# Linear attention, then RWKV channel mix: the weights of the gate load in two halves and those of the output product in five pieces, one group is mixed in halves, and the orders of all engines are new

## The chip, the cores and the metric

The kernel runs on one core of one Trainium2 chip. Every time is device time of one execution, in microseconds (us); smaller is better. The core has five engines that run beside each other, each working through its own list of instructions in order: TensorE (PE in the profile: matrix products and transposes, with weight loads, PEld, beside them), VectorE (DVE), ScalarE (ACT), GpSimd (POOL, which here mainly issues loads) and SyncE (SP, which here issues stores). Sixteen DMA engines move data between memory and the core. Products are gathered in PSUM, whose banks hold 512 float32 for each of 128 partitions.

## The reference

Two layers follow each other. The first is an attention without a square matrix. Its inputs q, k and v have 8 batches, 8 heads, 576 positions and 64 channels each:

```python
q_s = exp(q - max(q, axis=-1));  q_s = q_s / (sum(q_s, axis=-1) + 1e-09)   # over the channels
k_s = exp(k - max(k, axis=2));   k_s = k_s / (sum(k_s, axis=2) + 1e-09)    # over the positions
kv  = einsum('bhsd,bhse->bhde', k_s, v)
x   = einsum('bhsd,bhde->bhse', q_s, kv)     # then heads and channels side by side: (8, 576, 512)
```

The second is a channel mix. `x_prev` is x moved by one position, zero at the start of a batch:

```python
xk = mu_k * x + (1 - mu_k) * x_prev
xr = mu_r * x + (1 - mu_r) * x_prev
k  = relu(xk @ w_k)                 # 512 -> 1024
v  = (k * k) @ w_v                  # 1024 -> 512
out = v / (1 + exp(-(xr @ w_r)))    # 512 -> 512, the gate
```

## The kernel before

**Attention.** The work on q, k and v goes by batch b (0 to 7) and group g (0 or 1) of four heads, so there are sixteen such groups, written 00 to 71. For a group three loads of float32 go into one of eleven `raw` buffers each (`load30v0` is v of group 30). Batches 0 and 1 are loaded in halves of 288 KB (`load11k0`, `load11k1`; batch 0's v straight to bfloat16), the others whole, 576 KB. ScalarE takes the exponentials of q and k (`expq`, `expk`, L330) and casts v to bfloat16 (`cast`, L336); these are the last users of a raw buffer. VectorE sums the exponentials over the channels (`rsum`), takes reciprocals and scales q (`scale`). TensorE then runs a block: it transposes the scaled q in PSUM and forms kv (L399) with one column more for the sum over positions. The block is named `TKV20` where it stands alone and `B31` where the product q times kv of the group before it is in it. VectorE takes the reciprocal of the sum (`rz`, L406) and weighs kv (`w`); ScalarE copies the transposed q out (`qt`, L377). Where a group's x is formed alone, the product is named `X11`.

**Mixing.** ScalarE copies x out of PSUM: `xb` takes 512 positions (L545), `xs` the last 64 (L548), which lie in the bank of the neighbouring block. VectorE sets the moved edge (`edge`), takes the difference to the moved x (`diff`), scales it by mu (`sc`, one of each of two halves u of the channels and each of the two mixes) and adds the moved x (`mix310` for xk, `mix311` for xr of group 31). The results lie in two rings for four batches.

**Channel mix.** It goes by units of 512 positions (four and one of 256 to every four batches; 0 to 9), which need not end where a batch ends: unit 1 needs batches 0 and 1, unit 2 batches 1 and 2. A unit has eight tiles of 128 of the 1024 channels, `k00` to `k07` for unit 0 (four products each, L623), each followed by `relu` on ScalarE (L610, 512 columns) and `sq` on VectorE (L614). Then come four tiles of 128 positions: `r02` is the gate's product for tile 2 of unit 0 (four products of 512 columns, L655), `th02` its tanh on ScalarE (L660), `v020` and so on the output product in steps (L675), `o02` the gating on VectorE (L681), and two stores of 128 KB, issued by SyncE (`st`, L691). k, r and v share four banks of PSUM (`mm`). In units 0 and 1 the first four k tiles go in two steps, first the channels of one group (`k12`), then of the other (`k12.2`), so that they can begin before the second group is mixed.

**Weights.** POOL issues the loads of the weights (`weight`, L302), converted to bfloat16: `wk` in four pieces, `wr` whole, `wv` in the four pieces that the constant `WV` cuts (L31).

**The order of the work.** Nothing is scheduled by a program. `ORDER` (L44) lists every step once, and each engine issues its own steps in the order of that list; a step waits on its engine until what it needs is done, and everything behind it on that engine waits with it. The number behind a colon is the buffer that the step takes (`load30v0:0` takes raw buffer 0; `r22:1` takes bank 1 of `mm`); a step that takes a buffer waits until its last users are done. POOL issues loads in the order of the list too, and what is issued lands in that order. Where a bank holds two results that different engines read (`rz31` on VectorE and `xs30` on ScalarE read the same bank), the later one of the list waits for the earlier one:

```python
qt30 B31:1.0 relu20:2 ... k26:0 mix211 xs30:1 rz31:1 mix201 rrec400 ... r22:1 th22:1
```

The change touches `graph` with its inner functions `attention` and `unit`, the function that makes the weights' tiles, and `ORDER`.

Of the kernel before, what the change touches and what calls it, by code (L numbers as in the profile page):

```python
# [30 lines left out]
WV = (0, 2, 4, 6, 8)  # L31
# [49 lines left out]
load61v0:1 rsum500:1 v221 v201 k30:0 th23:3 k33:2 expq510:1 load60v0:10 expq410:0 relu33:2 o20
load61k0:3 relu30:1 v230:1 o22 w40:0 rsum410:2 sq30:1 rrec410 sc3110:2 cast410:1 sc3111 sc3011:1
k42:3 k43:2 relu43:0 rrec500 v231 sq33 expk410:1 o23 qt40:2 k47:0 v210:2 load51v0:9 v211 sc3010
scale410:0 relu42:1 sq42:0 k37:1 k40:3 load70v0:0 mix301 st20.2 expk500:2 relu40:2 cast500:2
B41:1.0 o21 rz41:0 k41:3 sq43 relu47:1 relu37:0 k31:2 w41:1 k34:0 scale500:1 sq40 xb40:1
load61q0:6 xs40 st23.2 sq47 mix311 relu41:2 relu34:1 qt41:0 k32:1 sq41 sq37 rsum510:3 sq34
relu31:2 r40:3 st22.2 relu32:0 k46:0 relu46:1 sq31 st20 st12 qt50:1 sq32 B50:0.1 sq46 rz50:1
# [765 lines left out]
```

## Time and profile before

Three runs took 195.58, 195.68 and 195.82 us; the median is 195.68.

| What | Value |
| --- | --- |
| Profiled execution, its own time | 195.74 us |
| Its span (first to last recorded work) | 194.0 us |
| Around the span | 1.74 us |
| TensorE busy | 183.8 us, 95%, 1807 instructions |
| Its weight loads | 89.8 us, 46%, beside the products |
| VectorE busy | 152.3 us, 79% |
| ScalarE busy | 139.4 us, 72% |
| POOL busy | 41.3 us, 21% |
| Granted clock of TensorE, mean | 0.996 |
| The chain that ended last | TensorE 67%, ScalarE 14%, VectorE 10%, waits for nothing shown 3%, DMA 3% |
| Read from memory, written | 33.56 MB, 9.44 MB |

The busy times are sums over the whole span and hide that it has two parts. Up to about 70 us all of the inputs of batches 0 to 3 have to come in (the DMA engines move 255 to 410 GB/s from 24 to 73 us) and ScalarE and VectorE are nearly full; later the transfers mostly stay under 230 GB/s and TensorE alone is full. A view of waits lists, for an engine, what ended its idle time: engine, operation, line, then what it waited for, with the sum, the number and the longest in us. In the listings of single instructions a row has the start (us from the start of the span), the duration, the engine, the line, the operation with its buffers and shape, and in brackets the idle time ahead of it with what ended it. The buffers' letters are those of the program: `raw_b` is the raw buffer 1, `mm_c` bank 2, `vv_c` the third buffer of casts. For a load, a row of the view of transfers gives the size and the time from issue to landing.

### The profile page before, as it was taken

To read this page: it belongs to the slowest core of one execution; us is meant where nothing else is said; L and a number is where in the kernel's file an instruction comes from. 1 tells how busy PE (TensorE), PEld (TensorE's weight loads), DVE (VectorE), ACT (ScalarE), POOL (GpSimd) and SP (SyncE) were. 2 spreads that over 40 slices of the span, in tenths; PEclk is the share of its full clock that TensorE was granted. 3 is DMA by queue.
4 is the path that set the end of the run, shared out by engine and by line. 5 is a ranking of instruction groups with operands and counts; after the bars stand their busy time and mean duration, and the time that the engine had idled before them with its cause. 6 is when DMAs were issued, how large, how long until landed. Compare 5 with 4: busy or idle time off the path is not lost.

```text
span 194.0 us, 4636 instructions
## 1 busy us (share of the span) xinstructions
PE 183.8 (95%) x1807; PEld 89.8 (46%) x1830; DVE 152.3 (79%) x353; ACT 139.4 (72%) x218; POOL 41.3 (21%) x65
## 2 busy tenths in 40 slices
PE   7798979999999989999999999999999999999991
PEld 2264434444544544555444444444444444444751
DVE  1888983999999999999999999999795824342531
ACT  3778999899999999999899969573444525141440
POOL 8345656544325202430020000000000000000000
PEclk9999999999999999999999999999999999999998
DMA  6999999999999999999996603911207003275813
GB/s 200 309 295 274 323 329 255 405 391 406 410 389 400 408 408 307 316 339 409 170 227 184 144 0 30 202 31 37 53 20 174 19 8 81 48 168 132 195 30 108
DMA packets 23614, 41.86 MB, mean 216 GB/s; under 512 B 9372, under 2 KB 12712, under 8 KB 23592
## 3 DMA queue, kind: packets, MB, share of 16 engines
q0 software_dynamic: 9392, 27.99, 43.9%
q1 hardware_dynamic: 13384, 12.14, 26.1%
q10 hardware_dynamic: 816, 1.44, 2.2%
q8 instruction: 14, 0.23, 0.5%
q14 instruction: 8, 0.07, 0.1%
HBM read 33.56 MB, written 9.44 MB: 222 GB/s over the span
## 4 chain that ended last, share of the span: by engine, by line
PE 67%; ACT 14%; DVE 10%; issue 3%; DMA 3%; SPq 1%; ACTq 0%; DVEq 0%
PE mm_b L675 8%; PE mm_c L675 7%; PE mm_d L675 6%; PE mm_c L623 6%; PE mm_d L623 6%; PE mm_a L623 6%; PE mm_b L623 5%; PE mm_a L675 4%; PE mm_a L655 4%; PE mm_d L655 3%; PE mm_c L655 3%; DMA mu_rows<-in_moe_mu_r_dram 3%; PE mm_b L655 2%; ACT rel_a L610 1%; ACT qt_c L377 1%
## 5 line engine op out<-in xcount | busy, mean ns | idle before, releaser
L675 PEld LDWEIGHTS <-k_a 128*128 128x128 bf16 x168 | 16.1, 98 | 17.3 <-issue 0.2
L655 PEld LDWEIGHTS <-xr 128*128 128x128 bf16 x144 | 13.6, 98 | 18.4 <-DMA wr<-in_moe_w_r_dram 1.5
L675 PEld LDWEIGHTS <-k_b 128*128 128x128 bf16 x128 | 12.1, 98 | 14.6 <-DVE k_b L614 0.3
L655 PE MATMUL mm_c<-wr,xr 128*128 128x512 bf16 x39 | 10.2, 380 | 1.4 <-DMA wr<-in_moe_w_r_dram 1.4
L623 PEld LDWEIGHTS <-wk_bb 128*128 128x128 bf16 x80 | 7.8, 98 | 7.8
L623 PEld LDWEIGHTS <-wk_ab 128*128 128x128 bf16 x80 | 7.8, 98 | 7.8
L655 PE MATMUL mm_a<-wr,xr 128*128 128x512 bf16 x44 | 11.3, 379 | 0.0
L623 PEld LDWEIGHTS <-wk_aa 128*128 128x128 bf16 x80 | 7.6, 98 | 7.9 <-issue 0.2
L623 PEld LDWEIGHTS <-wk_ba 128*128 128x128 bf16 x80 | 7.4, 97 | 7.6 <-DMA wk_ba<-in_moe_w_k_dram 0.2
L610 ACT ACTIVATE rel_b<-mm_a 128x512 bf16<-128x512 f32 (+1 forms) x11 | 5.7, 521 | 5.1 <-PE mm_a L623 4.9
L655 PE MATMUL mm_d<-wr,xr 128*128 128x512 bf16 x33 | 9.1, 380 | 0.2
L610 ACT ACTIVATE rel_a<-mm_d 128x512 bf16<-128x512 f32 (+1 forms) x11 | 6.6, 604 | 3.6 <-PE mm_d L623 2.4
L681 DVE SCALAR_TENSOR_TENSOR th_a<-th_a,mm_c 128x512 f32<-128x512 f32 x4 | 2.7, 687 | 8.2 <-PE mm_c L675 5.4
L610 ACT ACTIVATE rel_c<-mm_d 128x512 bf16<-128x512 f32 (+1 forms) x7 | 3.5, 504 | 6.7 <-PE mm_d L623 6.6
L623 PE MATMUL mm_d<-xk,wk_ab 128*128 128x512 bf16 (+1 forms) x30 | 8.1, 351 | 0.1
L614 DVE TENSOR_TENSOR k_a<-rel_a 128x512 bf16<-128x512 bf16 (+1 forms) x15 | 5.9, 392 | 2.8 <-ACT rel_a L610 2.6
L614 DVE TENSOR_TENSOR k_b<-rel_a 128x512 bf16<-128x512 bf16 x14 | 5.9, 421 | 2.7 <-ACT rel_a L610 2.7
L623 PE MATMUL mm_d<-xk,wk_aa 128*128 128x512 bf16 (+1 forms) x29 | 7.9, 350 | 0.0
L623 PE MATMUL mm_b<-xk,wk_bb 128*128 128x512 bf16 (+1 forms) x26 | 7.5, 371 | 0.1
L623 PE MATMUL mm_b<-xk,wk_ba 128*128 128x512 bf16 (+1 forms) x24 | 7.1, 371 | 0.1
L614 DVE TENSOR_TENSOR k_a<-rel_b 128x512 bf16<-128x512 bf16 (+1 forms) x17 | 6.2, 366 | 0.9 <-ACT rel_b L610 0.5
L345 DVE TENSOR_REDUCE rsum_a<-eq_a 128x9 f32<-128x576 bf16 (+1 forms) x4 | 4.1, 1050 | 3.5 <-ACT eq_a L330 3.5
(350 smaller groups left out, 539.4 us busy)
## 6 DMA issues: line engine op xcount, KB each, us to landing
raw_a<-in_v_dram POOLq DMA_DIRECT2D x3, 576.0 KB, 11.4
out_dram<-th_d SPq DMA_DIRECT2D x12, 128.0 KB, 2.4
out_dram<-th_a SPq DMA_DIRECT2D x12, 128.0 KB, 2.4
out_dram<-th_c SPq DMA_DIRECT2D x10, 128.0 KB, 2.5
out_dram<-th_f SPq DMA_DIRECT2D x10, 128.0 KB, 5.6
raw_k<-in_q_dram POOLq DMA_DIRECT2D x2, 576.0 KB, 9.9
raw_g<-in_k_dram POOLq DMA_DIRECT2D x2, 576.0 KB, 10.6
raw_f<-in_k_dram POOLq DMA_DIRECT2D x2, 576.0 KB, 12.3
```

What stands on the lines that cost most here:

```text
L345: return kn.nc.vector.reduce_sum(out=sums(kn.rsums, u), in_=kn.eqs[eq.index][:, :, u, :], axis=AX.X)
L377: kn.nc.scalar.copy(out=to[:, :, 64:64 + S], in_=kn.whole(slot).bitcast(BF16)[:, :, 0:S])
L610: kn.nc.scalar.activation(out=kn.rels[rel.index][:, 0:n], in_=kn.bank(kf)[:, 0:n], func=ACT.Relu, scale=HALF_ROOT)
L614: kn.nc.vector.tensor_tensor(out=kn.k2s[k2.index][:, fc, 0:n], in0=kn.rels[rel.index][:, 0:n], in1=kn.rels[rel.index][:, 0:n], op=ALU.mult)
L623: kn.nc.tensor.matmul(kn.bank(kf)[:, 0:n], lhsT=kn.wk[fc // 4][ct % 2][:, ct // 2, (fc % 4) * 128: (fc % 4) * 128 + 128], rhs=kn.xs[0][:, ...
L655: kn.nc.tensor.matmul(kn.bank(rps), lhsT=kn.xs[1][:, ct, c:c + 128], rhs=kn.wr[:, ct, :], start=(ct == 0), stop=(ct == CT - 1))
L675: kn.nc.tensor.matmul(kn.bank(vps)[:, 0:width], lhsT=kn.k2s[k2.index][:, ft, 128 * m:128 * m + 128], rhs=wv_of(ft)[:, part], start=(ft == ...
L681: kn.nc.vector.scalar_tensor_tensor(out=kn.ths[th.index][:, part], in0=kn.ths[th.index][:, part], scalar=1.0, in1=kn.bank(vps)[:, 0:width] ...
```

## The change

The load of w_r is two loads of two of its four pieces of 128 channels each, `wr0` and `wr1`, into two tiles, and the r products of unit 0 are two steps: `r02` with the first half for channels 0 to 255, `r02.2` with the second. The later units' r products keep one step and need both halves. The load of w_v has five pieces in place of four (the first two are one piece of 128 channels each, 128 KB as bfloat16), and unit 0's v products follow these cuts, five steps to a tile instead of four.

Group 11 is mixed in halves: `xb11` is two copies (`xb110`, `xb111`) of 512 columns, one for each half of the channels, `diff11` is two, and `mix110` is two (`mix1100`, `mix1101`); `mix111` stays one step. The second step of the first k tiles of unit 1 is cut in two likewise (`k12.2`, `k12.3`), each needing the half of the mix that it reads.

All of `ORDER` is written anew. Batch 1 is loaded q first (`load10q0` before `load10k1`); the order of the eight k tiles, four r tiles and of their relus in unit 0 differs; the whole loads of batches 2 and 3 come in another order, with `load30v0` behind `load50q0`, `load40q0`, `load50v0`, `load40v0` and `load31v0`; `load41v0` stands later, behind `expk510`, into raw buffer 5; ScalarE takes `cast310` before `cast300`; `mix201` stands before `rz31` and `rz31` before `xs30`. The buffers and banks of the steps differ with it. The number of raw buffers and all others stays. In the part of `ORDER` shown here the lines of before stand first, then those of after; the rest of it, for units 3 to 9, differs throughout as well.

```diff
-WV = (0, 2, 4, 6, 8)
+WV = (0, 1, 2, 4, 6, 8)
...
+SPLIT = ((1, 1),)
...
-warm load00k1 load01v late load01k0:3 load10k1:4 wk00 load10v1:5 expq001:0 expq000 wk01
-rsum001:0 ACT!load01k1 rsum000 load10q1:6 expq011:1 rrec001 load10q0 rrec000 rsum011:1 fill:1
...
-wp010:1 cast101:0 load10k0 k02:1 edge01 load10v0 X010:1.0 mucopy x0011 x0100 load11q1 wr k03:0
-expq101:2 expq100 k01:2 expk101:2 x0101 k00:3 k01.2 k02.2 load11v1:8 load11k1:9 k00.2 relu00:0
-k03.2 rsum101:2 wp011 X011:0.1 rsum100 load11k0 sq00:0 load11v0 relu01:1 rrec100 sq01 wv0
-relu02:2 k04:3 wv1 x0110 wv2 k06:2 rrec101 expq110:0 wv3 scale100:2 relu04:0 load20q0:10 expk100
-load30q0:0 load20v0:2 cast100 k07:1 k05:3 scale101 rsum110:3 sq04 rrec110 sq02 relu06:1 relu03:0
-load21q0:1 sq06 x0111 TKV10:0 load21v0:3 relu07:2 r02:2 r03:0 r00:1 rz10:2 load20k0:6 scale110:0
-expq111 relu05:1 w10:0 qt10:2 r01:3 cast111:1 rsum111 expk111:0 expk110 rrec111 scale111 cast110
-B11:1.0 sq03 th03:0 v030:0 th01:1 th00:2 xs10:0 v010:3 sq07 load31q0:4 xb10 rz11:0 w11:1 sq05
-edge10 diff10:0 qt11:0 v000:1 th02:3 v011 v001 sc1000:0 sc1001 v031 X11:0.1 sc1010:1 sc1011 v012
-load21k0:5 v032 v013 xs11:1 v002 mix100 xb11 v033 v003 edge11 expq200:1 diff11:1 expq300:2 o01
-load31k0:7 sc1101:2 v020:2 v021 v022 sc1100 o00 v023 mix110 load41q0:9 o02 rsum200:0 k11:3
-sc1111:0 k12:1 load31v0:8 k12.2 cast200:2 o03 mix101 k10:2 k11.2 k10.2 relu12:0 k16:1 expq210:0
-relu11:2 k17:0 relu16:1 sq12:1 sq11 relu10:0 sc1110 relu17:2 cast210:0 k13:3 rrec200 mix111 st02
-expk200:1 k15:1 k13.2 scale200:1 sq16 r11:2 load30k0:10 k14:0 rsum210:1 sq10 rrec210 TKV20:1
-rz20:1 sq17 relu13:1 load30v0:0 r12:3 th11:4 r10:2 w20:2 sq13 expk210:2 relu14:0 r13:0 qt20:1
-scale210:2 sq14 rsum300:2 load40k0:2 relu15:2 th12:5 sq15 B21:0.1 expq310:1 rz21:2 load51k0:1
-rrec300 v120:1 v110:3 w21:0 st01.2 st00 st02.2 xb20:0 scale300:0 st00.2 xs20 th13:6 load40q0:3
-edge20 qt21:2 rsum310:3 diff20:0 th10:3 v121 load40v0:6 sc2001:2 sc2000 v111 expk300:0 X21:1.0
-r20:0 v130:2 xs21:1 v131 rrec310 xb21 o11 v100:3 edge21 v101 mix200 diff21:1 load60k0:5 o12
-sc2101:1 sc2100 mix210 o10 st01 cast300:1 st03 TKV30:0 cast310:2 th20:2 expk310:1 load50v0:4
-expk400:2 load50q0:10 rz30:0 k27:1 sc2110:0 st11.2 sc2111 relu27:1 o13 expq400:0 w30:1 k20:0
-scale310:1 load41v0:0 load70q0:8 sq27:0 k21:3 relu21:0 k24:1 rsum400:0 k23:2 k22:3 qt30:0
-B31:1.0 relu20:2 sq20 sc2010:2 st11 st12.2 relu23:1 cast400:0 relu24:2 sc2011 sq21 relu22:0
-k26:0 mix211 xs30:1 rz31:1 mix201 rrec400 w31:2 k25:2 scale400:2 sq22 xb30 edge30 qt31:1 sq23
-load50k0:7 load60q0:2 load51q0:3 r22:1 th22:1 st10.2 relu25:0 sq24 diff30:1 r30:3 relu26:1
...
+warm load00k1 load01v late load01k0:3 load10q0:4 wk00 load10q1 expq001:0 expq000 load10k0:5
+rsum001:0 ACT!load01k1 rsum000 wk01 expq011:1 rrec001 wk11 rrec000 rsum011:1 fill:1 fill.2:2
...
+expk010:1 fill.19:3 fill.20:1 fill.21:1 T01:3 kvn00:0 load10v1:6 mu:0 load11q0:7 fill.22:1
+expk011 load10v0 edge00 load10k1 wp000:0 load11q1 wr0 X000:1.0 load11k1:8 wp001 mucopy qt01:1
+expq100:2 KV010:2 x0001 KV011 Z01 rz01:1 kvn01:1 wp010:1 edge01 wr1 load11k0 X001:0.3 x0000
+k01:0 k03:1 x0010 x0011 X010:1.0 x0100 k02:2 wp011 k00:3 x0101 rsum100:2 rrec100 X011:0.1 x0111
+scale100:2 expq101 expk100:2 k01.2 load11v0:9 k00.2 k03.2 rsum101 x0110 relu01:0 k02.2 load11v1
+relu00:1 wv0 wv1 relu03:2 cast101:0 k04:0 k07:3 sq01:0 k05:1 relu04:0 expq110:0 k06:0 rrec101
+cast100 expk101 expq111 scale101 sq00 rsum110:3 sq03 relu02:1 TKV10:0 r02:2 relu06:2 rrec110
+sq02 r01:0 relu05:1 r00:1 rsum111 sq04 expk111:0 rz10:2 wv2 w10:0 rrec111 relu07:0 scale111:0
+wv3 scale110 wv4 load30q0:10 r03:3 load20q0:0 load20v0:2 r01.2 qt10:2 r02.2 sq06 expk110
+load21q0:1 cast110:1 r03.2 r00.2 cast111 load21v0:3 th00:0 sq05 B11:1.0 th03:1 th02:2 xs10:0
+v030:1 v031 rz11:0 v000:3 v010:2 v011 v001 w11:1 sq07 xb10 edge10 qt11:0 v012 diff10:0 sc1000:0
+v032 v002 X11:0.1 xs11:1 th01:3 sc1001 v013 v003 v004 xb110 load20k0:4 v014 sc1011:1 v033 xb111
+load21k0:6 edge11 v020:0 v021 mix100 v034 sc1010 load30k0:5 v022 load50q0:7 v023 v024 diff110:1
+o00 k11:3 diff111 sc1110:2 o01 sc1100:0 expq300:1 sc1101 mix1100 k12:2 load31q0:8 expq200:2
+k12.2 mix1101 k12.3 o02 k11.2 rsum200:0 sc1111 o03 cast200:2 k11.3 k10:0 mix111 st00 relu12:2
+load40q0:9 sq12:1 k10.2 k10.3 relu11:1 sq11 rrec200 mix101 expq210:0 k17:2 k13:3 k13.2 k16:1
+load50v0:10 k13.3 relu10:0 scale200:1 sq10 cast210:0 k15:0 relu17:2 relu13:1 sq13 load40v0:0
+load31v0:2 r11:2 expk200:1 relu16:0 th11:4 r10:3 TKV20:1 rsum210:1 sq17 st03 st03.2 r13:1 k14:2
+load30v0:1 expk210:2 relu15:1 rrec210 rz20:1 w20:2 qt20:1 relu14:2 th13:5 load31k0:3 scale210:2
+r12:0 B21:0.1 v120:2 expq310:2 sq16 sq15 sq14 rsum300:2 rz21:2 st01 load40k0:4 xb20:1 v110:1
+w21:0 th10:6 rrec300 rsum310:3 xs20 qt21:2 v121 edge20 scale300:0 v130:3 load51q0:6 th12:1
+expk300:0 st02.2 load41k0:8 load51k0:5 st00.2 st02 diff20:0 X21:1.0 v111 o12 o11 sc2000:0 xb21:0
+v100:0 xs21 edge21 sc2001 r20:2 v131 cast310:1 cast300:2 diff21:1 v101 mix200 sc2100:2 sc2101
+mix210 sc2010:1 rrec310 o10 o13 TKV30:1 rz30:0 scale310:1 k27:1 th20:0 st13 w30:1 k24:2 k20:0
+sc2110:0 sc2111 expk310:1 expq400:0 expk400:2 relu27:0 relu20:1 k22:3 relu24:2 sq27:0 mix211
+sq24 k21:1 qt30:0 cast400:0 k23:0 relu22:0 st13.2 sc2011 B31:0.1 sq20 rsum400:0 mix201
+load41q0:2 k25:2 xb30:0 st12 k26:3 rz31:1 rrec400 relu21:2 r21:1 relu23:1 r22:0 w31:2 scale400:2
+xs30 qt31:1 th22:2 B40:1.0 sq22 sq21 sq23 load71q0:1 load61q0:3 relu25:0 edge30 diff30:1 v220:0
+load70v0:9 r23:2 st12.2 sc3000:2 xs31:1 relu26:2 load61v0:4 sq25 sq26 xb31 load51v0:0 th21:5
+rz40:2 expk410:0 r30:3 sc3001 edge31 diff31:0 st10.2 st11 st10 v200:1 v221 th30:1 sc3011:0
+sc3101:1 sc3100 expk510:1 mix300 th23:6 expq410:1 mix310 v201 load50k0:8 sc3110:2 o22 o20 k37:3
+k42:2 k30:0 rsum410:1 sc3111 relu37:1 expq500:2 rsum500:2 k33:1 sq37:1 rrec410 relu30:0
+load41v0:5 w40:0 st20.2 scale410:0 k43:3 k40:0 st22 st11.2 mix311 relu33:2 v230:1 expq510:0 v231
...
     wk_done = [[add("POOL", lambda h=h, g=g: weight(kn.wk[h][g], kn.w_k, F, g, 2, 2, 512 * h),
                     name=f"wk{h}{g}") for g in range(2)] for h in range(2)]
-    wr_done = add("POOL", lambda: weight(kn.wr, kn.w_r, C, 0, 1, CT, 0), name="wr")
+    wr_done = [add("POOL", lambda h=h: weight(kn.wr[h], kn.w_r, C, 2 * h, 1, 2, 0), name=f"wr{h}")
+               for h in range(2)]
     wv_done = [add("POOL", lambda i=i, a=a, e=e: weight(kn.wv[i], kn.w_v, C, a, 1, e - a, 0),
                    name=f"wv{i}") for i, (a, e) in enumerate(zip(WV, WV[1:]))]
...
-        def copy_first():
-            kn.nc.scalar.copy(out=kn.xbs[xb.index][:, :, 64:576], in_=kn.whole(pair))
+        halves = (slice(0, 1), slice(1, 2)) if (b, g) in SPLIT else (slice(0, 2),)
+
+        def copy_first(h):
+            kn.nc.scalar.copy(out=kn.xbs[xb.index][:, h, 64:576], in_=kn.whole(pair)[:, h, :])
...
         def then(made, other):
-            evs = [add("ACT", lambda: copy_second(other), [made], [xb], [other], name=f"xs{tag}"),
-                   add("ACT", copy_first, [made], [xb], [pair], name=f"xb{tag}")]
-            o = add("DVE", edge, evs + [late_consts], name=f"edge{tag}")
-            xdiff = add("DVE", diff, [o], [xd], name=f"diff{tag}")
+            last = add("ACT", lambda: copy_second(other), [made], [xb], [other], name=f"xs{tag}")
+            many = len(halves) > 1
+            firsts = [add("ACT", lambda h=h: copy_first(h), [made], [xb], [pair],
+                          name=f"xb{tag}{h.start if many else ''}") for h in halves]
+            o = add("DVE", edge, [last, late_consts] + ([] if many else firsts), name=f"edge{tag}")
+            diffs = [add("DVE", lambda h=h: diff(h), [o, f], [xd],
+                         name=f"diff{tag}{h.start if many else ''}")
+                     for h, f in zip(halves, firsts)]
             for m in range(2):
-                s = [add("DVE", lambda m=m, u=u: scale_x(m, u), [xdiff, mu_done],
+                s = [add("DVE", lambda m=m, u=u: scale_x(m, u), [diffs[u if many else 0], mu_done],
                          [xms[m]], [xd], name=f"sc{tag}{m}{u}") for u in range(2)]
-                mixed[b, g, m] = [add("DVE", lambda m=m: mix(m), s, [], [xms[m], xb], name=f"mix{tag}{m}")]
+                if many and m == 0:
+                    mixed[b, g, m] = [add("DVE", lambda m=m, h=h: mix(m, h), [s[h.start]], [],
+                                          [xms[m], xb], name=f"mix{tag}{m}{h.start}")
+                                      for h in halves]
+                else:
+                    mixed[b, g, m] = [add("DVE", lambda m=m: mix(m, slice(0, 2)), s, [],
+                                          [xms[m], xb], name=f"mix{tag}{m}")]
 
...
+                fine = any((b, 1) in SPLIT for b in bs)
+                for cts in (((0, 2), (1,), (3,)) if fine else ((0, 2), (1, 3))) if step == 4 else ((0, 2, 1, 3),):
                     gs = sorted({ct % 2 for ct in cts})
+                    ready = [o for b in bs for ct in cts
+                             for o in (mixed[b, ct % 2, 0][ct // 2:][:1] if (b, ct % 2) in SPLIT
+                                       else mixed[b, ct % 2, 0])]
                     for i in range(step):
                         fc = f1 + i
                         mms[i] = add("PE", lambda kf=kfs[i], fc=fc, cts=cts: k_part(kf, fc, cts),
-                                      [o for b in bs for g in gs for o in mixed[b, g, 0]]
+                                      list(dict.fromkeys(ready))
                                       + [wk_done[fc // 4][g] for g in gs] + [mms[i]],
                                       [kfs[i]] if cts[0] == 0 else [], [],
                                      name=f"k{index}{fc}")
...
-            def r_part(rps=rps, c=c):
-                for ct in range(CT):
+            def r_part(cts, rps=rps, c=c):
+                for ct in cts:
                     kn.nc.tensor.matmul(kn.bank(rps), lhsT=kn.xs[1][:, ct, c:c + 128],
-                                        rhs=kn.wr[:, ct, :], start=(ct == 0),
+                                        rhs=kn.wr[ct // 2][:, ct % 2, :], start=(ct == 0),
                                         stop=(ct == CT - 1))
...
             own = sorted({4 * half + c // S, 4 * half + (c + 127) // S})
-            r = add("PE", r_part,
-                     [o for b in own for g in range(2) for o in mixed[b, g, 1]] + [wr_done],
-                     [rps], [], name=f"r{index}{m}")
+            ready = [o for b in own for g in range(2) for o in mixed[b, g, 1]]
+            if index == 0:
+                r = add("PE", lambda f=r_part: f((0, 1)), ready + wr_done[:1], [rps], [],
+                        name=f"r{index}{m}")
+                r = add("PE", lambda f=r_part: f((2, 3)), wr_done[1:] + [r], [], [],
+                        name=f"r{index}{m}")
+            else:
+                r = add("PE", lambda f=r_part: f(range(CT)), ready + wr_done, [rps], [],
+                        name=f"r{index}{m}")
...
     kn.wv = [const.tile([128, e - a, C], BF16, name=f"wv_{x}")
-             for x, a, e in zip("abcd", WV, WV[1:])]
-    kn.wr = const.tile([128, CT, C], BF16, name="wr")
+             for x, a, e in zip("abcdefgh", WV, WV[1:])]
+    kn.wr = [const.tile([128, 2, C], BF16, name=f"wr_{x}") for x in "ab"]
```

More of the change, by code (lines that the diff above doesn't have):

```diff
@@ L81 @@
[L81 to L86, printed above, removed]
@@ new lines @@
+fill.13:1 fill.14:2 fill.15:3 fill.16:0 muload wide:0 scale000:0 expq010 expk000:0 rsum010
+expk001 scale001 widecopy wk10 rrec010 fill.17:1 fill.18:2 fill.23:3 fill.24:1 fill.25:2
+fill.26:3 fill.27:1 KV001:0 rrec011 scale010:1 KV000 T00:1 rest Z00 qt00:0 scale011 rz00:0
+expk010:1 fill.19:3 fill.20:1 fill.21:1 T01:3 kvn00:0 load10v1:6 mu:0 load11q0:7 fill.22:1
+expk011 load10v0 edge00 load10k1 wp000:0 load11q1 wr0 X000:1.0 load11k1:8 wp001 mucopy qt01:1
+expq100:2 KV010:2 x0001 KV011 Z01 rz01:1 kvn01:1 wp010:1 edge01 wr1 load11k0 X001:0.3 x0000
@@ new lines @@
+o23 sc3010 st01.2 relu42:1 sq30 v210:2 v211 o21 cast410:2 qt40:2 expk500:2 relu43:0 sq33 B41:0.1
+st21.2 st22.2 sq42:0 sq43 mix301 k41:1 k34:3 load60v0:2 k47:2 xs40:1 xb40 rrec500 relu41:2 sq41
+load60q0:7 relu34:1 relu40:0 k32:1 relu47:2 rz41:0 cast500:1 k46:3 w41:1 sq40 edge40 k36:0 st20
+k31:2 relu32:0 load70q0:6 load61k0:5 k44:1 sq34 relu46:1 scale500:1 sq32 qt41:0 relu36:0 sq46
+sq47 k35:3 rsum510:3 diff40:0 relu35:1 sq35 sc4001:1 r40:0 relu31:2 B50:1.0 st21 k45:3 th40:4
+relu44:1 xb41:0 sq31 sc4011:2 sc4000 r31:2 mix400 sq36 r33:0 v300:1 expq610:1 load71k0:8 th31:3
@@ L553, in edge, with diff @@
             kn.nc.vector.tensor_copy(out=t[:, :, 1:64], in_=t[:, :, 576:639])
-        def diff():
+        def diff(h):
             t = kn.xbs[xb.index]
-            kn.nc.vector.tensor_tensor(out=kn.xds[xd.index][:], in0=t[:, :, 64:64 + S],
-                                       in1=t[:, :, 0:S], op=ALU.subtract)
+            kn.nc.vector.tensor_tensor(out=kn.xds[xd.index][:, h, :], in0=t[:, h, 64:64 + S],
+                                       in1=t[:, h, 0:S], op=ALU.subtract)
         def scale_x(m, u):
@@ L564, in scale_x, with mix @@
                                        scalar1=kn.mu[:, c:c + 1], scalar2=None, op0=ALU.mult)
-        def mix(m):
-            kn.nc.vector.tensor_tensor(out=kn.xs[m][:, g::2, c0:c0 + S],
-                                       in0=kn.xms[xms[m].index][:],
-                                       in1=kn.xbs[xb.index][:, :, 0:S], op=ALU.add)
+        def mix(m, h):
+            kn.nc.vector.tensor_tensor(out=kn.xs[m][:, g::2, c0:c0 + S][:, h, :],
+                                       in0=kn.xms[xms[m].index][:, h, :],
+                                       in1=kn.xbs[xb.index][:, h, 0:S], op=ALU.add)
@@ L633, in unit @@
                 mms = [None] * step
-                for cts in ((0, 2), (1, 3)) if step == 4 else ((0, 2, 1, 3),):
+                fine = any((b, 1) in SPLIT for b in bs)
+                for cts in (((0, 2), (1,), (3,)) if fine else ((0, 2), (1, 3))) if step == 4 else ((0, 2, 1, 3),):
                     gs = sorted({ct % 2 for ct in cts})
+                    ready = [o for b in bs for ct in cts
+                             for o in (mixed[b, ct % 2, 0][ct // 2:][:1] if (b, ct % 2) in SPLIT
+                                       else mixed[b, ct % 2, 0])]
                     for i in range(step):
```

71 lines of the change are left out of this document (31 added, 40 removed).

## The prediction

> **What bounds the kernel now.** I read the waits of TensorE, the chain that ended last from 20 to 72 us, a table of busy time by stretch, then the rows of the places found. First, what TensorE waited for:
>
> ```profile
> PE mm_c L655 <- DMA wr<-in_moe_w_r_dram: 1.4, 1, 1.4
> ...
> PE mm_b L655 <- ACT xb_b L545: 0.7, 1, 0.7
> ...
> PE att_a L489 <- issue: 0.3, 1, 0.3
> ```
>
> After the start that is nearly all. The stretches (PE, PEld, DVE, ACT, POOL busy; clock; DMA share; GB/s):
>
> ```profile
> 24.50:31.00 6.50, 5.07 (x97) 2.60 (x98) 4.33 (x10) 6.38 (x12) 4.32 (x6) 1.00 1.15 299
> ...
> 39.00:56.00 17.00, 16.85 (x208) 8.05 (x210) 16.96 (x33) 16.56 (x23) 6.50 (x9) 1.00 1.04 401
> 56.00:71.00 15.00, 14.23 (x197) 6.67 (x201) 14.15 (x32) 14.70 (x21) 5.06 (x7) 1.00 1.03 403
> 71.00:189.00 118.00, 117.17 (x968) 57.88 (x982) 91.68 (x204) 76.91 (x126) 7.22 (x10) 1.00 0.55 142
> ```
>
> From 71 us TensorE alone is full. Before, ACT has 6.38 of 6.50 us just where TensorE waits for wr; from 39 to 56 DVE and ACT are both full. The chain there has no wait for wr:
>
> ```profile
> 26.92 1.12 ACT qt_c L377
> 28.04 0.58 ACT vv_b L336
> 28.62 1.15 ACT ek_a L330 x2
> 29.77 0.56 ACT vv_b L336
> 30.33 0.50 ACT th_a L660
> ```
>
> ACT then waits for three loads, one landing every 1.5 us, and does not again until 47:
>
> ```profile
> 36.09 1.16 ACT L330 ACTIVATE eq_b<-raw_k 128x1152 bf16<-128x1152 f32 x1 [0.48 <-DMA raw_k<-in_q_dram]
> 37.59 1.16 ACT L330 ACTIVATE eq_c<-raw_a 128x1152 bf16<-128x1152 f32 x1 [0.34 <-DMA raw_a<-in_q_dram]
> 39.10 1.15 ACT L336 CAST vv_c<-raw_c 128x1152 bf16<-128x1152 f32 x1 [0.34 <-DMA raw_c<-in_v_dram]
> ```
>
> So up to 69 us the end is set by ACT and by the line of loads; the wr wait is TensorE idling beside them.
>
> **The change, part by part.**
>
> *wr in halves.* The r products' four tiles take 3.46 us (four of 0.86). The wait of 1.38 goes, but r02, r01, r00, r03 need the banks that relu02, 06, 05, 07 free, and ACT gets there in its own order. From relu01 at about 19.6 (relu00 had 19.98): relus 0.48 a step, half casts and exponentials 0.57; 10v1 has the bytes in front of it that landed by 20.8 before, so nothing waits until expq111 (11q1, 24.2); relu02 ends at 25.4, relu06 25.8, relu05 26.3, then expk111 (landing 26.1), relu07 27.4. TensorE now waits for ACT: r03's first step starts at 27.4, four second steps of 0.43 end near 29.6, B11 starts there, not at 30.26. wr1 lands at about 27.4 (wr: 26.65), in time. KV11 needs cast111, whose load keeps the landing of the last one of batch 1, 29.55, so it starts at 30.3 to 30.6 for 31.00. Lead of TensorE: 0.4 to 0.7. ACT's queue holds the same from relu01 to the third tanh (8 relus, 9 half steps for 8 and one 0.53 copy, 1.05, three tanh: 11.46 us for 11.42), so the lead of ACT is 0.1 to 0.3.
>
> *wv in five pieces.* Same bytes; one more descriptor call on POOL (0.73, row wv_d 0.71), beside a line that lands one transfer per 0.7 to 1.5 us. wv0 to wv4 land at about 30.2, 30.8, 32.0, 33.3 and 34.5; the v steps reach them in that order and just wait for none: 0 to 0.2. I take 0.
>
> *Group 11 mixed in halves.* Two copies of 512 columns (0.48 a step) for one of 1024 (0.90): +0.06 on ACT. Two differences and two sums of 576 for 1152 (0.67): no such row; below by half (0.34), above by the 576-wide cast from PSUM (0.66): 0 to +0.6 for the two pairs; nearest are the 512-wide squares, also bf16, at 0.335, so +0.1. k12's odd steps gain the wait on half the sum only.
>
> All this lies ahead of the loads at 36.06, 37.57 and 39.07. The bytes ahead of them are the same, so ACT starts again at the same three times with the same work, and the lead is given back there. Worth at 39 us: 0 (bounds -0.3, +0.2).
>
> *The order of the loads.* The third batch's load30v0 was the 13th whole load; it is now the 15th, behind 50q0, 40q0, 50v0, 40v0 and 31v0. The 15th of before:
>
> ```profile
> 46.30 0.72 POOL L206 DMA_DIRECT2D raw_b<-in_k_dram  x1 [1.43 <-ACT ek_b L330]
> ...
> raw_b<-in_k_dram POOLq DMA_DIRECT2D x1, 576.0 KB, 12.7
> ```
>
> It landed at 46.30 + 12.7 = 59.0 with all seven stores of the first unit already paid. cast300 therefore starts at 59.0, where these rows show no wait:
>
> ```profile
> 57.08 1.25 ACT L336 CAST vv_b<-raw_a 128x1152 bf16<-128x1152 f32 x1
> 58.14 1.25 ACT L336 CAST vv_c<-raw_i 128x1152 bf16<-128x1152 f32 x1
> ...
> 59.88 0.48 PE L399 MATMUL att_a<-vv_b,ek_a 64*64 64x65 bf16 x36
> ```
>
> Behind cast300 on ACT stand th20, expk310, expq400, expk400, relu27, relu20, relu24, qt30: 59.0 + 1.05 + 0.49 + 3 x 1.05 + 3 x 0.48 + 1.0 = 66.1. KV30 starts at 60.2 for 59.88, and B31, which waits for qt30, at 66.3 for 65.57: +0.7.
>
> *The reciprocal rz31.* Before, rz31 stood behind the copy xs30 of the same bank, and mix201 behind rz31:
>
> ```profile
> 68.22 0.17 DVE L406 RECIPROCAL rz_b<-att_b 128x2 f32<-128x2 f32 x1 [0.68 <-ACT xb_b L548]
> ...
> 69.10 1.04 PE L655 MATMUL mm_b<-wr,xr 128*128 128x512 bf16 x4 [0.67 <-ACT xb_b L545]
> ```
>
> Now mix201 comes before rz31 and rz31 before xs30: -0.67. From B31 to B40 remain 70.93 - 65.57 - 0.67 = 4.69 us and a wait of some 0.1 for a freed bank: B40 at 71.1 for 70.93. Up to here: +0.2.
>
> *After 71 us.* The same products remain. 118.00 - 117.17 is 0.83, mostly records left out; one gap of 0.1 may go. New: load41v0 can be issued only when expk510 frees its buffer, about 76.6 by ACT's steps; the nearest row, issued at 76.67 (raw_k<-in_v), landed 5.5 later, so 82.1, and cast410's turn is at 81.8 to 82.3. 0 to 0.7, of which I take 0.15, as B41 follows with some products between.
>
> Sum: 0 + 0.7 - 0.67 + 0.1 + 0.15 - 0.05 = +0.25 on the profiled execution's 195.74 (span 194.0 and 1.74 around it): 195.99. The median shown is 0.06 lower: **195.95**. The bounds give 195.4 to 196.6.
>
> **A rule weighed.** The last two landings of batch 1's k halves (issued 19.84 and 21.12, 8.3 and 7.7 to landing: 28.1 and 28.8) are 0.7 us apart, so a transfer costs its bytes in this line. Whatever is fixed in a transfer's time in the line is under 0.7. [...]
>
> **Rivals.**
> 1. *The line of loads is not last (faster).* If load30v0 lands 0.5 us or more earlier than its place says, cast300 follows cast310 at 58.5, B31 starts near 65.8, and the 0.67 at r22 is a gain: -0.4, with a lead kept from the r products up to -0.9. For it: the wait on xb_b is plainly gone. Against: 13 landings in a row are 1.5 us apart or more. 195.0 to 195.4, say 195.2. Chance 0.22.
> 2. *load41v0 comes too late (slower).* Its place is the issue at 76 to 77; from a landing past 82.8 cast410 holds qt40 and expk500 up, and TensorE has B41 next: +0.4 to +1.2. For it: 5.5 us for the row issued at 76.67. Against: 4.2 for the one at 75.06. 196.4 to 197.2, say 196.7. Chance 0.24.
> 3. *The transfers have a fixed cost in the line (slower).* Two more of them, at most the 0.7 us of a whole landing each: load30v0 lands at 60.4, everything behind it 1.4 later, 197.3. For it: nothing separates bytes from calls at one size. Against: halves of 288 KB land 0.7 apart and whole loads of 576 KB 1.5, twice the bytes for twice the time. Chance 0.02.
> 4. *It does nothing:* ACT paces everything to 69 us whatever the order, and late loads have slack: 195.7. Chance 0.07.
>
> **How the numbers follow.** My forecast has 0.45; 0.2%, 0.39 us, is about what a measurement can tell from no change. Rival 1 gives 0.19 faster and 0.03 within; the forecast, with bounds from 195.4 to 196.6, 0.27 within and 0.18 slower; rival 4 0.07 within; rivals 2 and 3 slower with 0.26. Faster 0.19, within 0.37, slower 0.44. The range takes in rivals 1 and 2: 195.0 to 196.8.
>
> **What would show it.** No wait for wr; waits of TensorE at L674 (r) on ACT between 25 and 28 us; ACT idle for the loads of raw_c (31v0) and raw_b (30v0) at 57 and 59 us; KV30 at 60.2, B31 at 66.3; no 0.67 before r22; B40 near 71.1. The prediction is wrong if cast300 runs before 58.8, if the three waits at 36 to 39 us have moved, or if TensorE has more than 0.5 us of new gaps after 71 us.

## The result, and the profile after

Eight runs of the changed kernel took 197.37 to 198.12 us, median 197.67; eight of the kernel before have the median 195.69. The ratio is 1.0098, with a 95% interval of 1.0081 to 1.0116: slower by 1.9 us. The forecast was 195.95, with a range of 195.0 to 196.8: the time missed the forecast by 1.7 us and lies outside the range. The profiled execution took 197.56 us, its span is 195.8, 1.82 us over that of before.

Starts of single instructions show where the two traces part (us from the start of the span):

| Start of | Before | After | Difference |
| --- | --- | --- | --- |
| r02, first gate product | 26.70 | 25.50 | -1.20 |
| B11 | 30.26 | 29.90 | -0.36 |
| v030 | 31.41 | 31.05 | -0.36 |
| k11, first product of unit 1 | 38.80 | 38.64 | -0.16 |
| B31 | 65.57 | 66.52 | +0.95 |
| B40 | 70.93 | 71.28 | +0.35 |
| B41 | 84.99 | 85.82 | +0.83 |
| k90, first product of the last unit | 181.17 | 182.34 | +1.17 |
| last gating on VectorE | 190.06 | 191.24 | +1.18 |
| end of the span | 193.96 | 195.78 | +1.82 |

Up to B40 there is little. From B40 to the last gating the changed kernel loses 0.83 us more, and a last 0.64 us goes where no product is left. (That B41 also stands at +0.83 is chance: the new list puts fewer products between B40 and B41 and more behind B41, so the rows in between don't compare the same work.) What TensorE waited for in the changed kernel:

```profile
PE att_a L542 <- ACT qt_c L380: 1.0, 2, 0.8
...
PE mm_c L674 <- ACT rel_b L625: 0.5, 1, 0.5
PE mm_d L674 <- ACT rel_a L625: 0.5, 1, 0.5
PE att_b L402 <- ACT vv_c L339: 0.2, 1, 0.2
```

The waits for wr and for xb_b are gone. Two of 0.5 for banks that relus free (`rel`) stand in place of the first. At r02 the relu ends at 25.45 and wr0 landed at 25.43, so without the relu it would hardly start earlier. New is the wait of 0.8 us for the copy qt_c, which is qt40. The stretches (same columns as in the prediction):

```profile
24.50:31.00 6.50, 5.50 (x120) 2.67 (x114) 4.01 (x10) 6.50 (x12) 5.01 (x8) 1.00 1.17 277
39.00:56.00 17.00, 16.85 (x210) 7.96 (x208) 16.82 (x32) 16.27 (x23) 6.51 (x9) 1.00 1.04 400
56.00:71.00 15.00, 14.47 (x192) 6.97 (x190) 14.87 (x33) 14.46 (x20) 5.06 (x7) 1.00 1.03 397
71.00:189.00 118.00, 117.16 (x973) 57.23 (x972) 90.68 (x202) 76.45 (x127) 7.22 (x10) 1.00 0.53 144
```

In the first stretch TensorE is 0.43 us busier, and ScalarE is now busy for all of it. From 56 to 71 us ScalarE is idle 0.24 us more, where it waits for loads. In the last row TensorE is as busy as before (117.16 for 117.17), but the trace of before had only 1807 records of products, this one 1830. The idle 0.83 of before are many gaps of 0.05 us, as a record left out makes them, and one of 0.16; the 0.84 here are one gap, in front of B41. The chain of waits names it:

```profile
77.46 6.11 DMA raw_f<-in_v_dram
83.57 0.02 issue
83.60 1.15 ACT vv_c L339
84.75 1.03 ACT qt_c L380
85.78 0.04 issue
85.82 0.22 PE att_a L542 x4
```

`raw_f<-in_v` is load41v0: issued at 77.46, landed at 83.57. cast410 waits for it 0.98 us, qt40 stands behind the cast, and B41 behind qt40.

The end of the span is seen in the transfers from 190 to 197 us, by queue (packets, MB, share of 16 engines). Before:

```profile
q1 hardware_dynamic: 240, 0.26, 14.3%
q10 hardware_dynamic: 240, 0.26, 11.2%
```

After:

```profile
q1 hardware_dynamic: 240, 0.26, 14.4%
q10 hardware_dynamic: 240, 0.26, 11.0%
q14 instruction: 1, 0.01, 0.5%
```

The last stores are the same 240 packets on each of two queues. New is one packet of a queue that the profile calls instruction, 8 KB and 0.52 us on one of the DMA engines, at 193.05, while the last stores are on their way; before, that packet came at 185.88. From the start of the last gating to the end of the span it is 4.54 us for 3.90, and to the last landing of a store 3.33 for 2.68. Each store has sixteen landing records, and fifteen of the last store's are where they were, 2.74 us behind the gating for 2.67; one comes 0.58 later.

### The profile page after: what moved, and what is told of

It reads as the page before. It is cut to its first block, busy times and chain, and to the rows that moved or that the text cites. A ratio compares the mean times of both kernels' runs of the same rounds, so it can differ in the third digit from the quotient of the medians.

```text
span 195.8 us, 4659 instructions
## 1 busy us (share of the span) xinstructions
PE 186.1 (95%) x1830; PEld 90.3 (46%) x1830; DVE 152.8 (78%) x355; ACT 138.6 (71%) x219; POOL 42.4 (22%) x67
## 4 chain that ended last, share of the span: by engine, by line
PE 54%; DMA 20%; issue 8%; DVE 7%; ACT 6%; POOL 4%; POOLq 0%; DVEq 0%
PE mm_d L700 7%; DMA raw_b<-in_v_dram 7%; PE mm_a L638 6%; PE mm_c L700 6%; DMA raw_e<-in_q_dram 6%; PE mm_b L638 6%; PE mm_a L700 4%; PE mm_b L700 4%; PE mm_c L638 4%; DMA raw_h<-in_q_dram 4%; PE mm_d L638 4%; PE mm_a L674 4%; PE mm_b L674 3%; DMA raw_f<-in_v_dram 3%; PE mm_c L674 3%
## 5 line engine op out<-in xcount | busy, mean ns | idle before, releaser
L625 ACT ACTIVATE rel_a<-mm_b 128x512 bf16<-128x512 f32 (+1 forms) x8 | 4.6, 574 | 10.6 <-PE mm_b L638 9.9
L638 PE MATMUL mm_a<-xk,wk_aa 128*128 128x512 bf16 (+1 forms) x30 | 8.5, 365 | 0.5 <-ACT xk L502 0.5
L629 DVE TENSOR_TENSOR k_a<-rel_c 128x512 bf16<-128x512 bf16 (+1 forms) x17 | 6.4, 375 | 3.4 <-ACT rel_c L625 3.1
L629 DVE TENSOR_TENSOR k_b<-rel_c 128x512 bf16<-128x512 bf16 x11 | 4.6, 420 | 5.0 <-ACT rel_c L625 5.0
L638 PE MATMUL mm_a<-xk,wk_ab 128*128 128x512 bf16 (+1 forms) x30 | 8.5, 365 | 0.0
L625 ACT ACTIVATE rel_a<-mm_a 128x512 bf16<-128x512 f32 (+1 forms) x10 | 5.9, 592 | 3.0 <-PE mm_a L638 2.7
L674 PE MATMUL mm_c<-wr_a,xr 128*128 128x512 bf16 x22 | 6.5, 379 | 0.5 <-ACT rel_b L625 0.5
L674 PE MATMUL mm_c<-wr_b,xr 128*128 128x512 bf16 x22 | 6.5, 379 | 0.0
L674 PE MATMUL mm_a<-wr_b,xr 128*128 128x512 bf16 x22 | 6.5, 379 | 0.0
L674 PE MATMUL mm_a<-wr_a,xr 128*128 128x512 bf16 x22 | 6.5, 378 | 0.0
```

Of the source, the lines that this page charges most:

```text
L625: kn.nc.scalar.activation(out=kn.rels[rel.index][:, 0:n], in_=kn.bank(kf)[:, 0:n], func=ACT.Relu, scale=HALF_ROOT)
L629: kn.nc.vector.tensor_tensor(out=kn.k2s[k2.index][:, fc, 0:n], in0=kn.rels[rel.index][:, 0:n], in1=kn.rels[rel.index][:, 0:n], op=ALU.mult)
L638: kn.nc.tensor.matmul(kn.bank(kf)[:, 0:n], lhsT=kn.wk[fc // 4][ct % 2][:, ct // 2, (fc % 4) * 128: (fc % 4) * 128 + 128], rhs=kn.xs[0][:, ...
L674: kn.nc.tensor.matmul(kn.bank(rps), lhsT=kn.xs[1][:, ct, c:c + 128], rhs=kn.wr[ct // 2][:, ct % 2, :], start=(ct == 0), stop=(ct == CT - 1))
```

## The experiments

The times below are medians, and each ratio is to the kernel before on the same chip; the changed kernel has 197.67 and 1.0098.

**The late load and the end.** First the two losses that the table shows, singly and together.

```diff
-... v201 load50k0:8 ... relu30:0 load41v0:5 ...
+... v201 load41v0:8 ... relu30:0 load50k0:5 ...
```

> The changed kernel, with load41v0 and load50k0 exchanged in the line of loads (each takes the other's place and buffer); nothing else. Theory (the late load): v of group 41 lands at about 80.2 in place of 83.6, cast410 no longer waits (0.98 us), qt40 and with it B41 come 0.8 us earlier, the gap of 0.84 us of TensorE at 85.8 goes, and the time is 196.7 to 196.9 for 197.6. Load50k0 then lands at 83.6, ahead of expk500's turn at 85. Rival (ScalarE's own order in front of qt40 holds B41): the gap stays and the time is 197.6.

Measured: 196.70 us, ratio 1.0048 (1.0036 to 1.0060). ScalarE with load41v0 landed at 80.08:

```profile
82.24 0.38 ACT L623 ACTIVATE rel_b<-mm_c 128x256 bf16<-128x256 f32 x1
82.50 1.15 ACT L337 CAST vv_c<-raw_i 128x1152 bf16<-128x1152 f32 x1
83.54 1.13 ACT L378 COPY qt_c<-att_b 128x1152 bf16<-128x1152 bf16 x1
84.55 1.19 ACT L331 ACTIVATE ek_c<-raw_f 128x1152 bf16<-128x1152 f32 x1
```

The cast follows at once, B41 starts at 84.91 for 85.82, and the last product 0.98 us earlier. load50k0, which now lands at 83.53, is in time for expk500 (`ek_c`) at 84.55. So of the 1.98 us between the medians, 0.97 are the place of one load.

```diff
     def emit_warm():
+        for _ in range(8):
+            kn.nc.scalar.copy(out=kn.warm[:], in_=kn.warm[:])
         return kn.nc.scalar.activation(out=kn.warm[:], in_=kn.warm[:], func=ACT.Exp)
```

> The changed kernel with eight more copies of one element on ScalarE at its start, where it waits for its first load; nothing else. Theory (the end): the fetch of 8 KB of instructions that lies among the last stores at 193.05 belongs to ScalarE's list, which is shorter by some waits than before; with eight instructions more it comes some 5 to 7 us earlier, the stretch from the start of the last product's gating to the end of the span is 3.9 us for 4.5, and the time is 0.6 less: 197.0 for 197.6. Rival (the last stores are slow for another reason, such as the number of stores waiting): the stretch stays 4.5 us and the time 197.6.

Measured: 197.14 us, ratio 1.0067 (1.0050 to 1.0084). The packet of the queue instruction came at 187.0; from 190 to 197 us only the stores are left, and from the last gating at 191.55 to the end of the span at 195.44 it is 3.89 us:

```profile
q1 hardware_dynamic: 240, 0.26, 14.4%
q10 hardware_dynamic: 240, 0.26, 11.1%
```

With more instructions on ScalarE the median is 0.53 us lower. The intervals of the two ratios still overlap (the one begins at 1.0081, the other ends at 1.0084), so the time alone doesn't settle it; the next run does. (This profiled execution was late by 0.31 us already at B40, 71.59 for 71.28, so its span shows only part of the gain.) The packet moved with ScalarE's list, and the end with the packet. In all fourteen traces it comes when ScalarE has 320 to 322 records behind it. They agree on the end as well: where it fell at 192.0 to 193.1 (the changed kernel and the runs of the late load alone, of the two loads, of the four pieces and of the whole group) the stretch from the last gating is 4.5 to 4.8 us; in the eight others and the kernel before, with the packet at 185.5 to 187.4, it is 3.86 to 3.90.

A rival is that ScalarE itself is late: in the five traces it pauses 0.33 us ahead of its last store, for 0.04 in the nine. But counted from the gating, fifteen landings of that store are only 0.07 us later in the changed kernel; it is the sixteenth that is late, by 0.57 to 0.83 us in the five traces and by 0.01 in the nine. So one part of sixteen was held up. That it is the DMA engine which carried the packet fits, but the trace does not name the engine.

> Both edits together: load41v0 exchanged with load50k0, and eight more small copies at ScalarE's start. If the two losses are separate they add: 0.84 and 0.64 off 197.6, so 196.1 to 196.2, and what is left against the kernel before is the 0.35 us that B40 is late. If they have one cause, or either only moves the loss to a later place, the time stays above 196.5.

Measured: 195.97 us, ratio 1.0012 (1.0003 to 1.0020). 0.97 and 0.53 make 1.50, and together they took 1.70: neither hides the other. On top of the earlier load the copies are worth 0.73 us (195.97 for 196.70), and here the intervals are well apart. What is left is 0.3 us.

**The order of the loads.** Next, the step that the prediction held for the main loss.

```diff
-... v022 load50q0:7 ... relu12:2 load40q0:9 ... load31v0:2 ... load30v0:1 ...
+... v022 load30v0:7 ... relu12:2 load31v0:9 ... load40q0:2 ... load50q0:1 ...
```

> The changed kernel, with load30v0 exchanged in the line of loads with load50q0 and load31v0 with load40q0 (the buffers follow); nothing else. Theory (load30v0 as the fifteenth whole load holds cast300 and with it B31): v of group 30 lands at about 49 and of 31 at 53, ScalarE waits for neither, KV30 starts by 59.8 for 60.6, B31 at 65.6 to 65.9 for 66.5, and of these 0.6 to 0.9 us some 0.4 to 0.7 are left at B40, since the copy qt31 holds it next (it did so by 0.41 when the wait at r22 was taken from the kernel before). The time is 197.0 to 197.3 for 197.6. Rival (ScalarE and VectorE are full there whatever the loads do): B31 at 66.4 to 66.6 and 197.6.

Measured: 197.73 us, ratio 1.0112 (1.0093 to 1.0130): nothing gained. ScalarE:

```profile
57.26 1.21 ACT L337 CAST vv_b<-raw_j 128x1152 bf16<-128x1152 f32 x1
58.32 1.21 ACT L337 CAST vv_c<-raw_h 128x1152 bf16<-128x1152 f32 x1
59.37 0.66 ACT L677 ACTIVATE th_a<-mm_c 128x512 f32<-128x512 f32 x1
60.62 1.16 ACT L331 ACTIVATE ek_b<-raw_d 128x1152 bf16<-128x1152 f32 x1 [0.59 <-DMA raw_d<-in_k_dram]
```

Neither cast waits any more, but expk310 waits 0.59 us for load31k0, the next in the line, which lands at 60.54 here and at 60.65 in the changed kernel. B31 is at 66.40 for 66.52. The expected 65.6 to 65.9 was missed. Added to the two earlier edits, it gains nothing either, where 0.4 to 0.7 us were expected:

> The changed kernel with load41v0 exchanged with load50k0, eight more small copies at ScalarE's start, and load30v0 and load31v0 exchanged with load50q0 and load40q0. If the three are separate, the 195.97 of the first two together goes down by 0.4 to 0.7: 195.3 to 195.6, at or below the kernel before (195.7). Rival (line of loads not the cause of the late B31): 196.0.

Measured: 195.98 us, ratio 1.0019 (1.0010 to 1.0027). So the third load of batch 3 was moved as well, on top of these three edits:

```diff
-... k16:1 load50v0:10 ... th13:5 load31k0:3 ...
+... k16:1 load31k0:10 ... th13:5 load50v0:3 ...
```

> The kernel of the seventh run (load41v0 earlier, eight small copies, 30v0 and 31v0 exchanged with 50q0 and 40q0), and load31k0 exchanged with load50v0 too, so that all loads of batch 3 lie ahead of those of batches 4 and 5. Theory (the line of loads holds ScalarE load by load: with 30v0 and 31v0 early it waited 0.59 us for 31k0 instead): no wait for a load from 52 to 62 us, B31 at 65.7 to 66.0 for 66.4 to 66.7, B40 0.3 to 0.6 us earlier, and 195.3 to 195.7 for 195.98. Rival (VectorE or ScalarE is the limit there): 196.0.

Measured: 195.29 us, ratio 0.9979 (0.9970 to 0.9988): 0.69 us less than the run before it, and faster than the kernel before. ScalarE goes from the casts to expk310 without a wait:

```profile
59.03 1.21 ACT L339 CAST vv_c<-raw_h 128x1152 bf16<-128x1152 f32 x1
60.08 0.66 ACT L679 ACTIVATE th_a<-mm_c 128x512 f32<-128x512 f32 x1
60.57 1.22 ACT L333 ACTIVATE ek_b<-raw_k 128x1152 bf16<-128x1152 f32 x1
```

This profiled execution was late by 0.45 us already at X11 (34.61, for 34.16 in the run before it), so stretches are compared: from X11 to B40 it is 36.79 us for 37.29, half a microsecond less, and to B31 32.02 for 32.53 (B31 itself is at 66.63; the expected 65.7 to 66.0 was missed). That fits ScalarE held by the loads of batch 3 as a whole; what took the rest of the 0.69 the profile does not show.

It is only half of what B31 lost: in the changed kernel B31 comes 32.58 us after X11, before 31.47. A wait further ahead stays in all of these runs. expq310, before and in the changed kernel:

```profile
50.90 1.18 ACT L330 ACTIVATE eq_b<-raw_e 128x1152 bf16<-128x1152 f32 x1
```

```profile
51.11 1.16 ACT L333 ACTIVATE eq_c<-raw_i 128x1152 bf16<-128x1152 f32 x1 [0.48 <-DMA raw_i<-in_q_dram]
```

It waits for load31q0, which is the tenth of the whole loads in the new order and was the seventh before. Counted from X11 it starts 0.37 us later than before, 17.17 for 16.80, and no run moves that load.

**The reciprocal.** The one step that was forecast as a gain, alone in the kernel before:

```diff
-k26:0 mix211 xs30:1 rz31:1 mix201 rrec400 w31:2
+k26:0 mix211 mix201 rz31:1 xs30:1 rrec400 w31:2
```

> The kernel before, with rz31 put ahead of xs30 and mix201 ahead of rz31; nothing else. By the prediction's step the wait of 0.67 us in front of r22 goes and nothing is late in its place: the time is 195.0 to 195.2 for 195.7. Rival (ScalarE and VectorE are full there, so that another wait takes its place at r22, r30 or B40): 195.5 to 195.7.

Measured: 195.34 us, ratio 0.9980 (0.9972 to 0.9989), half of what was expected. TensorE's waits:

```profile
PE mm_c L653 <- ACT rel_b L608: 1.5, 1, 1.5
...
PE att_a L537 <- ACT qt_b L375: 0.4, 1, 0.4
```

The 1.5 is still the wait of r02 for wr, which landed at 26.69, 0.05 ahead of it; the view puts it down to the relu that freed the bank before. The wait of 0.67 at r22 is gone, and one of 0.41 for qt31 stands at B40: xs30 now starts only when rz31 has read the bank, at 68.36, and xb30 and qt31 come behind it. An order that lets xs30 start earlier:

```diff
-k26:0 mix211 xs30:1 rz31:1 mix201 rrec400 w31:2
+k26:0 rz31:1 w31:2 mix211 xs30:1 mix201 rrec400
```

> The kernel before, with rz31 and w31 ahead of mix211 and xs30 between mix211 and mix201. Theory (with the wait at r22 gone, the wait of 0.41 us at B40 for the copy qt31 took its place, since xs30 could only start at 68.36): xs30 starts at 67.8, qt31 ends at 69.9 to 70.0, r22 starts at 68.4 to 68.6 for 68.31, B40 at 70.2 to 70.4 for 70.61, and the time is 195.0 to 195.15. Rival (another step is late at B40): 195.3 to 195.4.

Measured: 195.27 us, ratio 0.9968 (0.9945 to 0.9991), not to be told from the run before it. The wait at B40 is gone, but mix201 is later by the two steps put ahead of it, so that 0.24 us of wait are back at r22 (68.83 for 68.31), and B40 is at 70.66 for 70.61. The expected 70.2 to 70.4 was missed, and the time too.

**The parts that were costed at nothing.** w_r in halves, in the kernel before:

```diff
-... load11q1 wr ... r01:3 ...
+... load11q1 wr0 wr1 ... r01:3 r02.2 r03.2 r00.2 r01.2 ...
```

> The kernel before, with the load of w_r in two halves at its old place in the line and unit 0's four r tiles in two steps (first all four first steps, then the four second steps); all orders else as before. Theory (ScalarE and the loads set the end up to 69 us): r02 starts at 25.4 to 25.5, when the first half has landed, for 26.70; the wait for wr goes, but B11, whose casts ScalarE reaches only then, starts at 29.8 to 30.3 for 30.26, and the three loads landing at 36 to 39 us take what is left: k11 within 0.1 of 38.80, and the time 195.6 to 195.8, no change. Rival (the wait of 1.38 us of TensorE is a loss): B11 and all behind it come about 1 us earlier, 194.5.

Measured: 195.80 us, ratio 1.0008 (0.9998 to 1.0017). TensorE from 25 us:

```profile
25.41 0.39 PE L654 MATMUL mm_c<-wr_a,xr 128*128 128x512 bf16 x1
...
29.35 0.22 PE L538 MATMUL att_b<-qt_c,w_a 64*64 64x64 bf16 x4
...
30.43 0.48 PE L398 MATMUL att_b<-vv_b,ek_a 64*64 64x65 bf16 x36 [0.27 <-ACT vv_b L335]
30.93 0.59 PE L680 MATMUL mm_a<-wv_a,k_a 128*128 128x512 bf16 x2
```

r02 starts 1.29 us and B11 0.91 us earlier; then kv of group 11 waits 0.27 us for ScalarE's cast, v030 is 0.48 ahead, k11 0.11, and B31 at 65.59 for 65.57 shows nothing of it. The largest wait of TensorE in the profile before, 1.38 us, was worth nothing.

w_v back in four pieces (`WV`, and four v steps to a tile), in the changed kernel:

> The changed kernel with w_v in four pieces as before, and unit 0's output products in four steps to a tile; nothing else. The prediction cost the fifth piece at nothing: B11, k11 and B40 within 0.1 us of the changed kernel's (29.90, 38.64, 71.28), and 197.5 to 197.8. Rival (each transfer costs something in the line of loads): every whole load lands up to 0.7 us earlier, load30v0 at 58.4 for 59.14, and up to 0.6 us of it reaches the end: 197.0.

Measured: 197.49 us, ratio 1.0102 (1.0088 to 1.0117); B11 30.00, k11 38.74, B40 71.25, load30v0 at 59.10 for 59.14. No cost and no gain can be told.

Group 11 mixed whole again (`SPLIT = ()`; one copy, difference and sum, `k12.2` in one step):

> The changed kernel with group 11 mixed whole again (one copy xb11, one diff11, one mix110) and the first k tiles of unit 1 in two steps; nothing else. The prediction cost the halves at nothing at the end: k12 within 0.2 us of 39.07, B40 within 0.1 of 71.28, 197.4 to 197.8. Rival (the halves are a gain that hides a part of the loss): k10 and r11 0.3 to 0.6 us later and 198.0.

Measured: 197.91 us, ratio 1.0106 (1.0089 to 1.0123); k12 39.05, k10 40.39, r11 44.77, B40 71.16, for 39.07, 40.37, 44.69 and 71.28. No difference.

**A late load put into the kernel before.** load41v0 and load60v0 exchanged, to see what a late load costs there (load70v0, the next load of one of the two buffers, follows to the other):

```diff
-... scale310:1 load41v0:0 ... expq510:1 load60v0:10 ...
+... scale310:1 load60v0:0 ... expq510:1 load41v0:10 ...
```

> The kernel before, with load41v0 exchanged with load60v0 (places and buffers), so that v of group 41 lands at 81.7 to 82.2, when cast410's turn on ScalarE is at 80.0; nothing else. Theory (a late load costs its lateness less the lead that the copy qt40 has on B41): qt40 ends at 83.4 in the kernel before and B41 starts at 85.0, a lead of 1.5; the cast is 1.7 to 2.2 late, so B41 is 0.2 to 0.7 late and the time 195.9 to 196.4. If lateness counted in full, 197.5; if ScalarE could not matter there, 195.7.

Measured: 197.43 us, ratio 1.0083 (1.0069 to 1.0097). ScalarE and TensorE:

```profile
82.00 1.15 ACT L334 CAST vv_b<-raw_k 128x1152 bf16<-128x1152 f32 x1 [1.82 <-DMA raw_k<-in_v_dram]
...
83.48 0.59 PE L673 MATMUL mm_c<-wv_a,k_a 128*128 128x512 bf16 x2 [1.40 <-ACT rel_a L608]
```

The theory was too mild. Not qt40 was held up first but the relu right behind the cast on ScalarE: it frees the bank that v210 takes, and TensorE stood still for 1.40 us at once. 1.82 us of lateness cost 1.54 us at k90; the lead of qt40 on B41 did not help.

## Why the prediction was wrong

The differences of the profiled executions add up: 0.35 to B40, 0.83 from there to the last gating and 0.64 behind it make 1.82. (The prediction's own sum has a slip that changes nothing: its terms add up to +0.23, not +0.25, and 195.99 less 0.06 is 195.93.) Of its three signs of being wrong the last one came: 0.84 us of new gap after 71 us.

*wr in halves: right.* Waits for banks that relus free took the place of the wait for wr, v030's lead was 0.36 (0.4 to 0.7 forecast, so just under it), and ScalarE started again at the same three landings:

```profile
36.16 1.17 ACT L333 ACTIVATE eq_b<-raw_k 128x1152 bf16<-128x1152 f32 x1 [0.21 <-DMA raw_k<-in_q_dram]
37.67 1.16 ACT L333 ACTIVATE eq_c<-raw_a 128x1152 bf16<-128x1152 f32 x1 [0.35 <-DMA raw_a<-in_q_dram]
39.18 1.15 ACT L339 CAST vv_c<-raw_c 128x1152 bf16<-128x1152 f32 x1 [0.34 <-DMA raw_c<-in_v_dram]
```

*wv in five pieces and the mixing in halves: right, 0 each* (the runs with either undone). wv0 and wv1, 128 KB each, landed at 30.12 and 30.77, 0.65 us apart and within 0.1 of the step. The third rival falls: with two transfers more, the three landings above are 0.07 to 0.09 later than before.

*The order of the loads: right in size, incomplete in cause.* load30v0 landed at 59.14 (59.0 forecast), kv of group 30 started at 60.37 (60.2), B31 at 66.52 (66.3). In the step load30v0 alone held ScalarE; taken away, load31k0 holds it almost as long, and load31q0 had held it already at 51 us. With the loads of batch 3 moved, about half of the lateness of B31 went; where the rest comes from was not shown, beyond the 0.37 us at expq310. The step asked what lands late and not what lands next.

*rz31: right in size in the changed kernel.* From B31 to B40 it is 4.76 us, 4.79 forecast. Alone in the kernel before, the same edit gains only 0.33, since the wait moves to qt31; in the changed kernel that wait is not there, and qt31 ends 0.2 us ahead of B40. Why, no run separates.

To B40 the sum was +0.2 and is +0.35. Two steps after it failed.

*load41v0: the term of 0.15 was 0.83.* It is the second rival, which had a chance of 0.24 and decided from a landing past 82.8; the landing was 83.57. Of the 1.5 us by which it came after the forecast landing, 0.9 are the issue (77.46, for 76.6: expk510, which frees the buffer, ran from 75.97, and POOL issued 0.3 after its end) and 0.6 the transfer (6.1 us, for the 5.5 of the nearest row). So the forecast landing failed first. What the step set against a late landing, the products between the cast and B41, failed too: 0.98 us of waiting cost 0.83 here, and 1.82 cost 1.54 in the kernel before, 85% both times.

*The end: no term at all, 0.64 in the trace and 0.53 in the medians.* The prediction took what lies behind the last product as given, though the new order changes the length of ScalarE's list. The list has 325 records for 332 of before, and 96 event waits for 104; the packet came with 3 records left, for 11 before, and so among the last stores.

The three losses undone together, with all else of the change kept, give 195.29 us, 0.2% faster than before: the change holds a gain of about 0.4 us under 2.4 us of side effects. That is the size of the first rival and not its mechanism, since load30v0 did not land early; it is near the 0.33 that rz31 gains alone, but no run shows that the two are the same.

## What to carry to other kernels

In this kernel a wait of the busiest engine was worth only what the next wait behind it left: 1.38 us of TensorE were worth nothing (195.80 us with w_r in halves, for 195.70 on that chip), because ScalarE and the loads set the time. When an order is written anew, list for each load its issue, its landing and the turn of its user; a load that is issued late, behind the release of its buffer, cost 85% of its lateness in both places tried, through what stands behind its user, while load50k0, put at the same late place, cost nothing, because its user's turn came later. Taking one late load away can hand the wait to the next one: with load30v0 early, expk310 waited 0.59 us for load31k0. Look at the stretch behind the last product too: it belongs to the time, and here it changed by 0.64 us in the trace, 0.53 in the medians, with the same packets and bytes of stores.

## What was not expected of the hardware

The traces show packets of the queue that the profile calls instruction among the transfers of the DMA engines: in the changed kernel 16 KB in 0.9 to 1.2 us each, 6 to 26 us apart, and 8 KB in 0.3 to 0.5 us eight times over the span. One of 8 KB among the last stores goes with 0.6 to 0.9 us more at the end, in all five traces that have it; eight added instructions on ScalarE moved it from 193.05 to 187.0 and took the median from 197.67 to 197.14 us, or from 196.70 to 195.97 with load41v0 early.
